# Attention in clusters and a softplus FFN: first batch by two heads, weight steps on either of two engines, one matmul for two in most similarities

## The chip, the cores and the metric

The kernel runs on one core of a Trainium2 chip. The core has a matrix engine (PE, with a weight load of its own, PEld), three engines for elementwise work (DVE, ACT, POOL) and a queue engine (SP); each takes its instructions in the order in which they were written, and they wait for each other by semaphores. DMAs are issued from the queues of ACT (loads) and SP (transposes and stores). PE writes only to PSUM, eight banks of 2 KB per partition; the other data lie in SBUF. The metric is the device time in microseconds, the median of several runs.

## The reference

Attention with 4 batches, 8 heads, 768 rows and a head size of 64, masked so that a query sees only the keys of its own cluster (16 centroids a head), then a feed-forward layer with softplus:

```python
q_assign = np.argmax(np.einsum('bhsd,hcd->bhsc', q_n, c_n), axis=-1)
k_assign = np.argmax(np.einsum('bhsd,hcd->bhsc', k_n, c_n), axis=-1)
mask = q_assign[:, :, :, None] == k_assign[:, :, None, :]
scores = np.where(mask, scale * np.matmul(q, k.transpose(0, 1, 3, 2)), -1000000000.0)
attn = softmax(scores)                      # minus the row's maximum, sum + 1e-9
x = np.matmul(attn, v)                      # then (4 * 768, 512)
h = x @ w_in                                # 512 to 2048
out = softplus(h) @ w_out                   # 2048 to 512
```

The inputs are float32, the two weights float64.

## The kernel before

Numbers are split into two float16 halves (a rounded value and what is left over), so that a float32 product is three float16 matmuls.

The work goes by *passes*: a batch has 6 blocks of 128 rows, a pass takes 3 of them for all 8 heads, so there are 8 passes, two a batch. A pass has 24 *tiles* (head by block). For a tile, `scores` (L529) makes the scores in PSUM (`s`, 4 matmuls at L544), takes the row's negative maximum on DVE (L560), and the exponential on ACT (L568). In pass 0 the result `p` is transposed by PE in float32 (`pT`, L585), copied out by ACT and DVE (L591, L593), and `attend` (L629) multiplies it with the raw v (L647). In later passes ACT rounds `p` (L607), POOL subtracts (L609, `phl`), a DMA transposes two tiles at a time, and L651 to L653 multiply. Two heads make a pair: DVE divides (L678), ACT and POOL split (L685, L687, `xn`), and a DMA transposes to `xT`.

Behind that runs the FFN of each pass: `ffn1` (L706) makes 16 column blocks `h` (L720 to L722), `softplus` (L731) turns them into `gh` through DVE (L739, L751), ACT (L741, L742, L762) and POOL (L763), and `ffn2` (L769) makes the output (L784 to L786) for two halves of the columns, with `store` (L793) behind it. `ffn1(0)` needs the `xT` of all four pairs of pass 0.

*Preparation.* `prep_k` (L412) takes two heads: load, split (ACT L423, POOL L425, `kn`), transposes (`turn`, L365: by PE and L376 in batch 0, by DMA from then on), `nearest` (L385: 12 blocks of two accumulating matmuls each, L394 and L395, with 16 columns, then four short DVE operations L399 to L403), a mask behind the copy of k in `n2`, and transposes again. `clusters` (L452) finds by a matmul with ones which clusters have any key at all (`alive`, event `al`). `prep_q` (L467) does the like for four heads and the 3 blocks of a pass; it waits for `kn` of the next pair before its load, and ahead of `nearest` for `al` of all four heads. `scores` waits for k of its pair and q of its four heads.

*Weights.* The float64 weights are made float16 halves in 32 steps (`prep_weights`, L270): 16 for `w_in`, 16 for `w_out`. A step loads 128 x 512 numbers, and then: ACT takes the absolute value of the high word scaled (L303), DVE shifts it left by 3 (L305), joins the sign (L309) and the upper bits of the low word (L315), ACT rounds (L318), POOL subtracts (L319). The raw words lie in rooms of `wo` that are still free.

*Order.* No hardware or compiler orders this. A planner in Python (`Order`, L28) runs all the generators against a model of the engines: each `op` names its engine and a duration, the planner takes the operation that can start first (then by priority, a number in units of tiles), and emits it. So every engine's queue has the order of the model. `ring(tag, n)` makes a generator wait until a buffer of n is free; `shared=True` keeps DVE and POOL operations of that kind apart in the model. In PSUM, `ps_s` has two buffers of two banks, `ps_h` two, `ps_o` and `ps_m` one each.

Of the kernel before, what the change touches and what calls it, by code (L numbers as in the profile page):

```python
# [19 lines left out]
DDS = 1024  # L20
LAG = 4
AHEAD = 10
NPE = 8
# [4 lines left out]
class Order:  # L28
# [8 lines left out]
    def __init__(self):  # L37
        self.free = dict.fromkeys(self.LAT, 0.0)
        self.ev, self.blocked, self.active = {}, {}, []
        self.dma = 0.0  # L40
        self.shared = {"DVE": 0.0, "POOL": 0.0}
        self.rings = {}
        self.cur, self.seq = None, 0
# [7 lines left out]
    def get(self, tag, size):  # L51

        k = self.rings.get(tag, 0)
        self.rings[tag] = k + 1
        return ("wait", (tag, k - size)) if k >= size else None, (tag, k)
# [23 lines left out]

    def run(self):  # L80
        while self.active:
            best = None
            for ch in self.active:
                _, eng, ns, _, opt = ch["op"]
                start = max(ch["now"], self.free[eng])
                if opt.get("shared"):
                    start = max(start, self.shared["POOL" if eng == "DVE" else "DVE"])
                prio = ch["prio"]() if callable(ch["prio"]) else ch["prio"]
                key = (start, prio, ch["seq"])
                if best is None or key < best[0]:  # L90
                    best = key, ch
            (start, _, _), ch = best
            self.active.remove(ch)
            _, eng, ns, emit, opt = ch["op"]
            self.free[eng] = start + ns
            if opt.get("shared"):
# [12 lines left out]
def tile_cluster_attention__then__softplus_ffn(  # L109
# [18 lines left out]
    SH = S // 2  # L128
    QT = 3

    passes = [(b, c0) for b in range(B) for c0 in range(0, NT, QT)]
    NF = DFF // P
    SCALE = 1.0 / math.sqrt(D)
    nb = QT * P

# [66 lines left out]

    def load(dst, src, nbytes):
        return op("ACT", 60, lambda: nc.scalar.dma_start(dst, src), dma=nbytes / 290.0)

    def flip(dst, src, blocks):

        return op(
            "SP", 150 * blocks + 100, lambda: nc.sync.dma_start_transpose(out=dst, in_=src), dma=180.0 * blocks
# [5 lines left out]
    def prep_centroids():  # L215
# [8 lines left out]
        yield op("DVE", 150, lambda: V.tensor_tensor(sq, cf, cf, ALU.mult), dma=0)  # L224
# [45 lines left out]
    def prep_weights(step: int):  # L270
# [30 lines left out]
        if f >= 0 and f // 2 in rooms:  # L301
            yield wait("wr", rooms[f // 2])
        yield op("ACT", 630, lambda: nc.scalar.activation(mag, val, AF.Abs, scale=sc))  # L303
        od.set(("wd", step))
        yield op("DVE", 420, lambda: nc.vector.tensor_scalar(mab, mab, 3, None, ALU.logical_shift_left), shared=True)  # L305
        yield op(
            "DVE",
            680,
            lambda: nc.vector.scalar_tensor_tensor(high, high, -0x80000000, mab, ALU.bitwise_and, ALU.bitwise_or),  # L309
            shared=True,  # L310
        )
# [6 lines left out]
        yield op("ACT", 610, lambda: nc.scalar.copy(part[:, 0], val))  # L318
        yield op("POOL", 1160, lambda: nc.gpsimd.tensor_tensor(part[:, 1], val, part[:, 0], ALU.subtract), shared=True)  # L319
# [11 lines left out]
    def raw_tile(nm, n, shape):  # L331

        if n < H and nm != "q":
# [3 lines left out]
        return key, p2.tile(shape, F32, tag="raw", name=f"raw{nm}_{n}")  # L337

    raw_v = {}

    def prep_v(n: int):
# [10 lines left out]
        yield op(  # L352
            "POOL",
            1640,
            lambda: nc.gpsimd.tensor_tensor(vb[:, :, :, :D], vf, vb[:, :, :, D : 2 * D], ALU.subtract),
            shared=True,
        )
# [7 lines left out]
    def turn(dst, src, name: str, on_chip: bool):  # L365
# [4 lines left out]
        for g in range(0, dst.shape[1], NT):  # L370
            hk = yield from ring("h", 2)
            ps = ps_h.tile([P, NT, P], F16, tag="h", name=f"{name}_{g}")

            def emit(g=g, ps=ps):
                for c in range(NT):
# [3 lines left out]
            if g:  # L379
                yield op("DVE", 950, lambda g=g, ps=ps: nc.vector.tensor_copy(dst[:, g : g + NT], ps))  # L380
            else:
# [500 lines left out]
```

## Time and profile before

| | us |
|---|---|
| median of 3 runs | 907.32 |
| lowest, highest | 904.31, 907.42 |
| the profiled execution | 904.0 |
| its span, first to last instruction | 902.2 |

Views of the profile used below: the page's busy times; the busy time of each engine by stretches; groups of instructions by line (count, total busy time, mean of one, idle time of the engine just before them and who ended it); the timeline (start, length, engine, line, operands); the waits by engine; and the chain of waits that ended last. PE's matmuls overlap each other, so the time that one adds is read from the distance of two starts, not from its length.

### The profile page before, as it was taken

The page shows a single profiled execution, that of the slowest core. Times are in us where ns is not written, and L with a number is a line of the kernel's source. Part 1 is how long each engine was busy: PE and PEld are TensorE (multiplying, and loading weights), DVE is VectorE, ACT ScalarE, POOL GpSimd, SP SyncE. Part 2 cuts the span into 40 slices and gives each one's busy share as a digit, 9 for nine tenths or more (in the row PEclk, how much of TensorE's full clock was granted, in tenths as well). Part 3 has the DMA queues.
Part 4 walks back from the last instruction along what each step waited for, and adds up shares of the span by engine and source line. Part 5 has one row for each costly group of instructions (what it writes and reads, how often), then busy time and mean ns, then how long its engine had stood idle before and what let it go on. Part 6 is the DMA issues. An engine that isn't in the chain of part 4 may idle for free.

```text
span 902.2 us, 19238 instructions
## 1 busy us (share of the span) xinstructions
PE 823.7 (91%) x7843; PEld 520.0 (58%) x7843; DVE 560.8 (62%) x1034; ACT 589.4 (65%) x904; POOL 523.9 (58%) x353
## 2 busy tenths in 40 slices
PE   2669797889679999999999999999999999999996
PEld 2558684555335666666666666666666666655542
DVE  5889787778685665675766666666665645433331
ACT  5657477886458877876767777867677676633320
POOL 5233326896548778777677676776676565512210
PEclk9979699999799999999999999999999999999998
DMA  6323439999546979999888779998867755600000
GB/s 222 95 94 120 130 128 195 199 226 237 141 123 159 202 171 202 223 203 230 157 199 179 162 149 206 207 211 182 171 155 161 133 115 138 126 9 25 12 1 35
DMA packets 393320, 136.02 MB, mean 151 GB/s; under 512 B 369680, under 2 KB 386064, under 8 KB 393232
## 3 DMA queue, kind: packets, MB, share of 16 engines
q1 hardware_dynamic: 371472, 99.15, 54.9%
q10 hardware_dynamic: 21760, 35.66, 13.0%
q8 instruction: 61, 1.00, 0.5%
q14 instruction: 27, 0.22, 0.1%
HBM read 35.68 MB, written 6.29 MB: 47 GB/s over the span
## 4 chain that ended last, share of the span: by engine, by line
PE 72%; DMA 4%; DVE 3%; POOL 3%; issue 2%; ACT 2%; POOLq 0%; DVEq 0%; ACTq 0%
PE s L544 10%; PE o L786 9%; PE o L784 9%; PE o L785 9%; PE h L720 8%; PE h L722 8%; PE h L721 8%; PE av L651 3%; PE av L653 3%; PE av L652 3%; DMA pt<-phl 3%; POOL phl L609 2%; DMA xT<-xn 1%; ACT p L568 1%; DVE negm L560 1%
## 5 line engine op out<-in xcount | busy, mean ns | idle before, releaser
L609 POOL TENSOR_TENSOR phl<-p,phl 128x768 f16<-128x768 f32 x168 | 277.2, 1666 | 90.9 <-ACT phl L607 54.2
L560 DVE TENSOR_REDUCE negm<-s 128x1 f32<-128x768 f32 x192 | 182.9, 954 | 67.5 <-PE s L544 65.2
L568 ACT ACTIVATE p<-s,negm 128x768 f32<-128x768 f32 x192 | 172.3, 898 | 72.9 <-DVE negm L560 47.7
L763 POOL TENSOR_TENSOR gh<-fg,gh 128x768 f16<-128x768 f32 x64 | 105.7, 1652 | 134.5 <-ACT gh L762 134.0
L720 PE MATMUL h<-xT,wi 128*128 128x384 f16 x512 | 167.9, 328 | 14.6 <-DVE fg L751 6.2
L722 PE MATMUL h<-xT,wi 128*128 128x384 f16 x512 | 168.1, 328 | 0.0
L721 PE MATMUL h<-xT,wi 128*128 128x384 f16 x512 | 168.0, 328 | 0.0
L544 PE MATMUL s<-kt,qt 128*128 128x384 f16 x768 | 158.5, 330 | 10.2 <-ACT p L568 10.0
L784 PE MATMUL o<-wo,gh 128*128 128x512 f16 x384 | 146.3, 381 | 4.9 <-ACT gh L762 3.3
L786 PE MATMUL o<-wo,gh 128*128 128x512 f16 x384 | 146.5, 382 | 1.4 <-POOL gh L763 1.4
L785 PE MATMUL o<-wo,gh 128*128 128x512 f16 x384 | 146.4, 381 | 0.1
L741 ACT ACTIVATE fa<-fa 128x384 f32<-128x384 f32 x128 | 66.6, 521 | 114.8 <-DVE fa L739 114.1
L607 ACT CAST phl<-p 128x768 f16<-128x768 f32 x168 | 134.1, 827 | 7.1 <-DMA pt<-phl 5.5
L739 DVE TENSOR_SCALAR fa<-h 128x384 int32<-128x384 int32 x128 | 71.1, 556 | 104.0 <-PE h L722 102.8
L651 PE MATMUL av<-vb,pt 128*128 128x65 f16 x1008 | 108.7, 192 | 1.9 <-DMA pt<-phl 1.8
L652 PE MATMUL av<-vb,pt 128*128 128x64 f16 x1008 | 108.7, 192 | 0.0
L653 PE MATMUL av<-vb,pt 128*128 128x65 f16 x1008 | 108.4, 194 | 0.0
L544 PEld LDWEIGHTS <-qt 128*128 128x128 f16 x768 | 72.7, 99 | 58.5 <-issue 15.1
L751 DVE SCALAR_TENSOR_TENSOR fg<-h,fa 128x384 f32<-128x384 f32 x128 | 70.6, 552 | 57.1 <-ACT fa L742 54.5
L651 PEld LDWEIGHTS <-pt 128*128 128x128 f16 x1008 | 93.6, 98 | 15.7 <-DMA pt<-phl 3.4
L652 PEld LDWEIGHTS <-pt 128*128 128x128 f16 x1008 | 92.9, 97 | 11.8
L653 PEld LDWEIGHTS <-pt 128*128 128x128 f16 x1008 | 93.1, 97 | 0.0
(114 smaller groups left out, 1193.6 us busy)
## 6 DMA issues: line engine op xcount, KB each, us to landing
wo<-in_moe_w_in_dram ACTq DMA_DIRECT2D x16, 512.0 KB, 3.6
wo<-in_moe_w_out_dram ACTq DMA_DIRECT2D x14, 512.0 KB, 3.9
rawk<-in_k_dram ACTq DMA_DIRECT2D x16, 384.0 KB, 4.8
rawv<-in_v_dram ACTq DMA_DIRECT2D x16, 384.0 KB, 4.8
rawq<-in_q_dram ACTq DMA_DIRECT2D x16, 384.0 KB, 4.2
out_dram<-ot SPq DMA_DIRECT2D x24, 256.0 KB, 2.5
pt<-phl SPq DMA_TRANSPOSE x84, 5.5
wraw<-in_moe_w_out_dram ACTq DMA_DIRECT2D x2, 512.0 KB, 3.7
```

Of the source, the lines that this page charges most:

```text
L544: nc.tensor.matmul(st[:, j, :SH], qt[:, s, i], kt[:, s, NT // 2 * j : NT // 2 * (j + 1)], start=(s == 0), stop=(s == 1),)
L560: yield op("DVE", 950, lambda: nc.vector.tensor_reduce(negm, st[:, :, :SH], AX.XY, ALU.max, negate=True))
L609: "POOL", 1640, lambda: nc.gpsimd.tensor_tensor(phl[:, u, 1], p32, phl[:, u, 0], ALU.subtract), shared=True
L651: nc.tensor.matmul(av, pt[:, 0, c], vb[:, c, D : 2 * D + 1], start=(c == 0), stop=False)
L652: nc.tensor.matmul(av[:, :D], pt[:, 0, c], vb[:, c, :D], start=False, stop=False)
L653: nc.tensor.matmul(av, pt[:, 1, c], vb[:, c, D : 2 * D + 1], start=False, stop=(c == NT - 1))
L720: nc.tensor.matmul(hp, w[0], x[0], start=(c == 0), stop=False)
L721: nc.tensor.matmul(hp, w[0], x[1], start=False, stop=False)
L722: nc.tensor.matmul(hp, w[1], x[0], start=False, stop=(c == NP - 1))
L784: nc.tensor.matmul(po, g[0], wo[:, f, 0, 0], start=(f == f0), stop=False)
L785: nc.tensor.matmul(po, g[0], wo[:, f, 0, 1], start=False, stop=False)
L786: nc.tensor.matmul(po, g[1], wo[:, f, 0, 0], start=False, stop=(f == f0 + NF // 2 - 1))
```

## The change

It has these parts.

1. **First batch by two heads.** `first_q` loads q for four heads without the wait for `kn` and spawns `prep_q` twice, for two heads each; `scores` in pass 0 waits for its two. In pass 0 `prep_q` waits for `al` only ahead of the last steps that use it. k and its mask in batch 0 share one tile of 192 columns (`kn12`, in buffers of `xT` and `phl`), which saves the copy L431. The PSUM tiles of this preparation may take any of the four pools (`EARLY`), those of `pT` two (`PTB`).
2. **Either of two engines.** An operation may name two engines, and the planner takes the one that ends sooner, with a handicap in ns: copies out of PSUM (`evict`: ACT or DVE), subtractions of a split (`sub`: POOL or DVE, handicap 2000 for DVE), and the weight steps (scale on ACT or POOL, sign on DVE or POOL, rounding on ACT or DVE). Where POOL makes the sign it multiplies by 0.0, and L309's successor shifts and joins in one operation.
3. **Weight steps by tiles.** Step s waits for the scores of tile int(1.4 s).
4. **One matmul for two** in 8 of the 12 blocks of `nearest` after batch 0 (k) and after pass 0 (q): one matmul with 32 columns (both halves of the centroids side by side) in place of two accumulating ones with 16, and one DVE sum of 256 columns for the eight.
5. **The last `xT` of pass 0** is transposed by PE in place of the DMA.
6. The planner's model: loads and DMA transposes have queues of their own, and several durations differ. `clusters` counts on the mask itself.

The core of the diff:

```diff
+FIRST = 3
+SLACK = 0
+BIAS = 2000
+WBIAS = -500
+EARLY = "homs"
+PTB = "ho"
...
+                    _, ns, eng = min((self.start(ch, e) + n + (e != eng[0]) * ch["op"][4].get("bias", 0), n, e) for e, n in zip(eng, ns))
...
-            if "dma" in opt:
-                self.dma = max(self.dma, start + 900) + opt["dma"]
-                end = max(self.dma, start + ns) + 1500
+            if "flip" in opt:
+                self.flips = max(self.flips, start + 900) + opt["flip"] * (2.0 if self.loads > start else 1.0)
+                end = max(self.flips, start + ns) + 1200
+            if "load" in opt:
+                self.loads = max(self.loads, start + 1200) + opt["load"] * (2.0 if self.flips > start else 1.0)
+                end = self.loads + 1200
...
+    def evict(dst, src, size):
+        return op(
+            ("ACT", "DVE"),
+            (180 + size * 0.8, 160 + size * 1.04),
+            (lambda: nc.scalar.copy(dst, src), lambda: nc.vector.tensor_copy(dst, src)),
+        )
+    def sub(dst, a, b, size):
+        return op(
+            ("POOL", "DVE"),
+            (150 + size * 1.95, 120 + size * 1.08),
+            [lambda e=e: e.tensor_tensor(dst, a, b, ALU.subtract) for e in (nc.gpsimd, nc.vector)],
+            shared=True,
+            bias=BIAS,
+        )
...
-        yield op("ACT", 630, lambda: nc.scalar.activation(mag, val, AF.Abs, scale=sc))
+        gate = int(WGATE + step * WPACE)
+        if gate >= 0:
+            yield wait("sc", gate)
...
+            if e == "ACT":
+                nc.scalar.activation(mag, val, AF.Copy, scale=sc)
+            else:
+                nc.gpsimd.tensor_scalar(mag, val, sc, None, ALU.mult)
+        yield op(("ACT", "POOL"), (630, 1000), [lambda e=e: scaled(e) for e in ("ACT", "POOL")], shared=True, bias=WBIAS)
...
+            if e == "POOL":
+                nc.gpsimd.tensor_scalar(val, val, 0.0, None, ALU.mult)
+            else:
+                nc.vector.tensor_scalar(mab, mab, 3, None, ALU.logical_shift_left)
+        yield op(("DVE", "POOL"), (420, 1000), [lambda e=e: signed(e) for e in ("DVE", "POOL")], shared=True, bias=WBIAS)
+        def joined():
+            if how[1] == "POOL":
+                a, x, f, b = mab, 3, ALU.logical_shift_left, high
+            else:
+                a, x, f, b = high, -0x80000000, ALU.bitwise_and, mab
+            nc.vector.scalar_tensor_tensor(high, a, x, b, f, ALU.bitwise_or)
...
+                if c < twin:
+                    nc.tensor.matmul(both[:, c], x, cents[:, 0 : low + 1 : low, h], start=True, stop=True)
+                    continue
                 nc.tensor.matmul(sim[:, c], x, cents[:, 0, h], start=True, stop=False)
                 nc.tensor.matmul(sim[:, c], x, cents[:, low, h], start=False, stop=True)
...
+    def first_q(n: int):
+        qkey[n, 0] = yield from ring("qt", 2)
+        nt = passes[0][2]
+        rk, qf = yield from load_q(n, 0)
+        qt = p2.tile([P, 2, 4, nt, P], F16, tag="qt", name=f"qt_{n}_0")
+        for u in range(4):
+            qT[n + u, 0] = qt[:, :, u]
+        for u in (0, 2):
+            od.spawn(prep_q(n + u, 0, 2, qf[:, u : u + 2], qt[:, :, u : u + 2], rk if u else None), od.cur["prio"] + u * nt)
...
-        yield wait("q", n - n % 4, pi)
+        yield wait("q", n - n % (4 if pi else 2), pi)
...
-        yield flip(
-            xT[pi][:, pr].rearrange("p s c t -> p (s c) t"), t_.rearrange("p s c d -> p (s c d)"), 2 * QT
-        )
+        yield from turn(
+            xT[pi][:, pr].rearrange("p s c t -> p (s c) t"),
+            t_.rearrange("p s c d -> p (s c) d"),
+            f"xT_{pr}_{pi}",
+            pi == 0 and pr == NP - 1,
+        )
```

More of the change, by code (lines that the diff above doesn't have):

```diff
@@ L78, in pump, with start @@
         self.cur = outer
+    def start(self, ch, eng):
+        t = max(ch["now"], self.free[eng])
+        if ch["op"][4].get("shared") and eng in self.shared:
+            t = max(t, self.shared["POOL" if eng == "DVE" else "DVE"])
+        return t
     def run(self):
         while self.active:
-            best = None
+            ready = []
             for ch in self.active:
[L84 to L87, printed above, removed]
+                eng, ns = ch["op"][1:3]
+                if isinstance(eng, tuple):
+                    _, ns, eng = min((self.start(ch, e) + n + (e != eng[0]) * ch["op"][4].get("bias", 0), n, e) for e, n in zip(eng, ns))
@@ L88, in run @@
                 prio = ch["prio"]() if callable(ch["prio"]) else ch["prio"]
[L89 to L92, printed above, removed]
+                ready.append((self.start(ch, eng), prio, ch["seq"], eng, ns, ch))
+            soon = min(ready, key=lambda r: r[:3])
+            start, _, _, eng, ns, ch = min(
+                (r for r in ready if r[3] == soon[3] and r[0] <= soon[0] + SLACK), key=lambda r: (r[1], r[0], r[2])
+            )
@@ L317, in prep_weights @@
         )
-        yield op("ACT", 610, lambda: nc.scalar.copy(part[:, 0], val))
-        yield op("POOL", 1160, lambda: nc.gpsimd.tensor_tensor(part[:, 1], val, part[:, 0], ALU.subtract), shared=True)
+        yield op(
+            ("ACT", "DVE"),
+            (610, 620),
+            (lambda: nc.scalar.copy(part[:, 0], val), lambda: nc.vector.tensor_copy(part[:, 0], val)),
+            shared=True,
+        )
+        yield sub(part[:, 1], val, part[:, 0], WC)
         od.set(("wr", step))
@@ L433, in prep_k @@
         h = n % H
         yield wait("cents")
-        hk = yield from ring("h", 2)
-        ps, sim, best = yield from nearest(
-            [kt0[:, c] for c in range(2 * NT)], [h] * NT + [h + 1] * NT, 2, f"k{n}"
-        )
-        eq = p2.tile([P, 2 * NT, NCL], F16, tag="eq", name=f"eq_k{n}")
-        yield op("DVE", 345, lambda: nc.vector.tensor_tensor(eq, sim, best, ALU.is_equal))
-        yield op(
-            "DVE",
-            250,
-            lambda: nc.vector.tensor_scalar(n2[:, :, D : D + NCL], eq, 1.0, MASK, ALU.subtract, ALU.mult),
-            shared=True,
-        )
@@ L447, in prep_k @@
-        od.spawn(clusters(n, ps, eq, hk), od.cur["prio"])
-        yield from turn(kt[:, 1].rearrange("p h c t -> p (h c) t"), n2, f"kT1_{n}", n < NPE)
-        od.set(n2k)
+        hk, ps = yield from bank(EARLY if n < H else "h", [P, 2 * (TWIN + NT), NCL], F32, f"sim_k{n}")
+        sim, best = yield from nearest(
+            ps, [kt0[:, c] for c in range(2 * NT)], [h] * NT + [h + 1] * NT, 2, f"k{n}", TWIN * (n >= H)
+        )
+        yield op("DVE", 345, lambda: nc.vector.tensor_tensor(sim, sim, best, ALU.is_equal))
@@ L450, in prep_k, with clusters @@
+        mask = n2[:, :, D : D + NCL]
+        yield op("DVE", 345, lambda: nc.vector.tensor_scalar(mask, sim, 1.0, MASK, ALU.subtract, ALU.mult))
+        od.spawn(clusters(n, ps, mask, hk), od.cur["prio"])
+        yield from turn(kt[:, 1].rearrange("p h c t -> p (h c) t"), n2, f"kT1_{n}", n < H)
+        for key in keys:
+            od.set(key)
         od.set(("k", n))
[L452 removed]
+    def clusters(n, ps, mask, hk):
         h = n % H
[L455 to L456 removed]
+        cnt = ps[:, : 2 * NT]
+        yield op("PE", 100, lambda: nc.tensor.matmul(cnt, ones, mask, start=True, stop=True))
```

300 lines of the change are left out of this document (164 added, 136 removed).

## The prediction

> **What bounds the kernel now.** I read the page's first line of busy times, then the busy time by stretches. Its columns: the stretch, its length, the busy time of PE, weight load, DVE, ACT and POOL (instructions in brackets), granted clock, DMA share, GB/s.
>
> ```profile
> PE 823.7 (91%) x7843; PEld 520.0 (58%) x7843; DVE 560.8 (62%) x1034; ACT 589.4 (65%) x904; POOL 523.9 (58%) x353
> ...
> 0.00:28.00 28.00, 9.57 (x110) 7.91 (x111) 16.20 (x61) 15.78 (x23) 14.71 (x17) 1.00 0.54 181
> 28.00:53.00 25.00, 12.70 (x181) 10.99 (x180) 21.87 (x54) 12.44 (x19) 7.93 (x6) 0.85 0.37 119
> 53.00:135.00 82.00, 72.76 (x543) 61.25 (x542) 71.63 (x116) 54.08 (x109) 22.93 (x20) 0.88 0.40 119
> 135.00:225.00 90.00, 76.15 (x828) 48.30 (x826) 68.78 (x115) 70.21 (x107) 71.58 (x47) 1.00 1.03 213
> 225.00:270.00 45.00, 30.49 (x259) 17.68 (x258) 32.05 (x66) 23.08 (x37) 20.67 (x14) 0.85 0.51 131
> 270.00:870.00 600.00, 599.29 (x5838) 364.23 (x5837) 344.84 (x618) 409.41 (x606) 382.82 (x248) 1.00 0.74 154
> ```
>
> The 91% of the first row hides two different stages. From 270 to 870 us PE is busy for 599.29 of 600 us at clock 1.00, and no other engine is over 70%: only less PE work brings time there. Before 270 us PE is idle for 270 - (9.57 + 12.70 + 72.76 + 76.15 + 30.49) = 68.3 us, and part of what it does runs at 0.85 to 0.88. All of PE's work has to be done at some time, so an idle microsecond saved before 270 comes off the end. Nearly the whole question lies in these 270 us.
>
> What holds PE there? The timeline of PE, around the first scores and at the end of pass 0:
>
> ```profile
> 44.02 0.17 PE L395 MATMUL sim_q<-cents,qt 128*128 128x16 f16 x1
> ...
> 44.52 0.17 PE L395 MATMUL sim_q<-cents,qt 128*128 128x16 f16 x1
> 49.85 0.82 PE L376 MATMUL qT<-eye,n 128*128 128x128 f16 x6 [5.16 <-POOL n L516]
> ...
> 54.03 2.27 PE L544 MATMUL s<-kt,qt 128*128 128x384 f16 x8
> ...
> 133.05 1.45 PE L647 MATMUL av<-rawv,ptf 128*128 128x64 f32 x12
> 134.33 0.50 PE L585 MATMUL pT<-eye,p 128*128 128x128 f32 x3
> 134.67 0.81 PE L544 MATMUL s<-kt,qt 128*128 128x384 f16 x4
> 135.32 1.45 PE L647 MATMUL av<-rawv,ptf 128*128 128x64 f32 x12
> ```
>
> The first scores come at 54.03 us, after the preparation of four heads. The 24 tiles of pass 0 then take until 135, 3.4 us each. By the starts in the last four rows PE needs 1.28 us a tile for `av`, 0.34 twice for `pT` and 0.65 for `s`: 2.61, or 63 us for 24. So PE alone does not set this stage; DVE is nearly full (21.87 of 25 us, 71.63 of 82). Its groups from 20 to 135 us (count, busy us, mean ns, idle before):
>
> ```profile
> L560 DVE TENSOR_REDUCE negm<-s 128x1 f32<-128x768 f32 x25 | 23.6, 948 | 3.8 <-PE s L544 3.6
> L315 DVE SCALAR_TENSOR_TENSOR wo<-wo 128x512 int32<-128x512 int32 x21 | 17.6, 836 | 0.2
> ...
> L309 DVE SCALAR_TENSOR_TENSOR wo<-wo,wi 128x512 int32<-128x512 int32 x16 | 12.4, 775 | 0.3
> L305 DVE TENSOR_SCALAR wi<-wi 128x512 int32<-128x512 int32 x16 | 10.0, 626 | 0.1
> L309 DVE SCALAR_TENSOR_TENSOR wo<-wo 128x512 int32<-128x512 int32 x5 | 3.5, 694 | 0.4
> ...
> L305 DVE TENSOR_SCALAR wo<-wo 128x512 int32<-128x512 int32 x5 | 2.1, 421 | 0.8 <-ACT wo L303 0.8
> ```
>
> Weight steps take 17.6 + 12.4 + 10.0 + 3.5 + 2.1 = 45.6 us of DVE for 21 steps, more than the scores' own reduction. That is the load the change touches.
>
> **The change part by part.** First, stage 1, up to the end of pass 0.
>
> *Start by two heads.* In the run of before, the first pair of k heads has its last transposes and copy here, and q is loaded late:
>
> ```profile
> 11.93 0.37 ACTq L204 DMA_DIRECT2D rawq<-in_q_dram  x1
> ...
> 22.95 0.80 PE L376 MATMUL kT<-eye,n 128*128 128x128 f16 x6 [0.89 <-ACT kt L382]
> ...
> 23.78 0.80 ACT L382 COPY kt<-kT 128x768 f16<-128x768 f16 x1 [0.89 <-PE kT L376]
> ```
>
> k of heads 0 and 1 is thus ready at 24.6 us. With q loaded without the wait for `kn`, prepared for two heads, and waiting for `al` only ahead of its last steps, the first scores can follow at about 28 us instead of 54. That saves no work: the other three k pairs and q halves now run between tiles. It fills PE's and POOL's idle time of 28 to 53 us. Halving q doubles its short DVE operations (two more sets of nine; at half the columns each is some 0.25 instead of 0.35 us, so 0.15 a pair is lost): 2.7 us on DVE.
>
> *Weight steps.* Step s now waits for tile int(1.4 s), so 17 steps fall into pass 0's tiles instead of 21; the sign may go to POOL, which leaves two DVE operations. The units, with L315's shortest, median and longest, and one of the short operations:
>
> ```profile
> L315 DVE SCALAR_TENSOR_TENSOR wo<-wo x30: 677/693/2159, 25.9 to 257.9; 128x512 int32<-128x512 int32 x30
> ...
> L319 POOL TENSOR_TENSOR wi<-wo,wi 128x512 f16<-128x512 f32 x16 | 18.7, 1170 | 58.2 <-ACT wi L318 58.2
> ...
> L303 ACT ACTIVATE wi<-wo 128x512 f32<-128x512 f32 x16 | 10.8, 678 | 6.1 <-DMA wo<-in_moe_w_in_dram 6.1
> ...
> L170 POOL CAST eye<-eye 128x128 f32<-128x128 f16 x1 | 0.3, 290 | 0.1
> ...
> L399 DVE TENSOR_REDUCE mx_q<-sim_q 128x12 f32<-128x192 f32 x16 | 5.6, 352 | 4.0 <-PE sim_q L395 4.0
> ```
>
> POOL's product with a number on 512 columns is not in the trace. Four times L170 gives 1.16 us, L319 with its two inputs 1.17; a cost per element below L170's, if some of that is start-up, could bring 0.6. I take 1.0, as the nearest row is L170. On DVE a step costs between 2 x 0.69 = 1.4 us (sign on POOL, nothing waits) and 45.6 / 21 = 2.2 (as now); I take 1.7. DVE's load up to 135 us is 16.20 + 21.87 + 71.63 = 109.7; it becomes 109.7 - 45.6 + 17 x 1.7 + 2.7 = 95.7. DVE was idle for 28 - 16.20 = 11.8 us at the start, which stays, and I leave 6 us of later waiting (it had 82 - 71.63 = 10.4 after 53 us): pass 0 ends at 95.7 + 18 = 114 instead of 135. PE's need fits under that: 9.57 + 12.70 of preparation and 63, in 114 us. **Stage 1 gains 21 us.** Ends: 8 (each step as dear as 2.2, and 10 us more waiting) and 30 (1.4 a step, and as much PE work as 95% of the time after 28 us can hold).
>
> *The last `xT` of pass 0 by PE.* The chain of waits holds the DMA transpose, and PE's wait list for 135 to 290 us shows what it cost:
>
> ```profile
> 144.97 8.12 DMA xT<-xn
> ...
> PE s L544 <- ACT p L568: 8.9, 9, 1.8
> PE h L720 <- DVE fg L751: 6.2, 4, 3.3
> PE h L720 <- DVE aq L511: 5.4, 1, 5.4
> PE h L720 <- DMA xT<-xn: 2.9, 1, 2.9
> ```
>
> Of the 8.12 us PE idled 2.9, the rest lay under score and `av` work. Six transposes (0.80 in the row at 22.95) and two copies replace it: 0 to 8 us, and I take **2.9**.
>
> *One matmul for two.* Twelve k and fourteen q preparations lose 8 matmuls each, 208 in all. Twenty starts lie between 44.02 and 44.52, 25 ns each, and with 32 columns one is still at the short end. 208 x 0.025 = **5.2 us** off PE, nearly all in the full stretch. The added DVE sum (26 on 256 columns, 0.47 us each by L399's 352 ns on 192) lies beside PE there, where DVE has 345 of 600 us; without that cover it would cost 12. That covers as well the copies and splits that may now run on either engine.
>
> *Pass 1 and the change of batch*, 135 to 270 us: 15 weight steps are left instead of 11, free to use any engine, while `phl`, `gh` and `kn` splits may leave POOL when it is behind. The new order may close some of the waits listed, or make others. Ends: 14 gained (half of the idle 135 - 76.15 - 30.49 = 28.4) and 40 lost (below); I take 0, as the load per engine stays near what it is.
>
> Sum: 21 + 2.9 + 5.2 + 0 = 29 us. The profiled execution took 904.0 us with a span of 902.2, which is the low end of the three runs (904.3 to 907.4, median 907.3). 904.0 - 29 = **875 us**; against the median it would be 878.
>
> **The rivals.** *DVE is held by POOL.* L315 takes 677 ns at best and 836 on average over the 21 above, though POOL is busy for only 22.93 of 82 us. The excess, with L309's 775 - 694 and L305's 626 - 421, is 0.45 us a step. With 17 steps of up to 3.2 us (1.0 + 1.0 + 1.17) POOL would be busy for some two thirds of the stage, 2.4 times the share, and two operations would then wait 1.1 us a step: DVE 2.5 a step, 13 us more than my 1.7. Gain 8 + 2.9 + 5.2: 888 us. The Trainium skill, SBUF — State Buffer, "SBUF: two separate sides", says that DVE in some modes and GpSimd take one pair of ports by an exclusive lock for a whole instruction, so that the other waits; by that rule the steps handed to POOL come back as DVE waits. The trace agrees in kind (677 against 2159 ns for one form), not yet in amount.
>
> *The change of batch closes too.* If k and q of batch 1 come early enough, the 14 us come on top: 861 us, or 852 if stage 1 also gives 30. For it: the waits on `fg` and `aq` are queue order, not load. Against it: k of batch 1 still waits for the buffers of batch 0.
>
> *POOL becomes the bound of pass 1 (slower).* The stretch again, for L319 alone (length, POOL's busy time):
>
> ```profile
> 135.00:225.00 90.00, 8.10 (x7) 1.00 1.03 213
> ```
>
> POOL has 71.58 of 90 us there, of which L319 is 8.1. Fifteen steps at 3.2 us are 48: 111 us of POOL, and with the idle 18.4 kept the stage lasts 130 instead of 90. 904 - 29 + 40 = 915 us. It decides from 29 us more POOL work, (29 + 8.1) / 15 = 2.5 us a step, that is when POOL does more than half of both optional operations. Against it: either engine may take them.
>
> *It does nothing measurable.* The first q half still comes only after all k heads, because of queue order, and pass 1 gives back the DVE relief: 900 to 910.
>
> **How the numbers follow.** Forecast (862 to 884) 0.46; DVE held 0.18 (884 to 900); the change of batch too 0.20 (848 to 862); nothing 0.06; slower 0.10. The range 851 to 902 leaves out the slower case, the nothing case's upper part and a sliver below: 2 in 10. About 0.5% of 907.3, 4.5 us, is what a measurement of this kernel can tell from no change. Faster 0.84, same 0.06, slower 0.10.
>
> **What would show it.** Right: first scores near 28 us, pass 0's last near 114, PE full from some 245 us on, sim matmuls 208 fewer. Wrong: first scores after 40; L309 and L315 means over 1.0 us (DVE held); POOL over 95% between pass 0 and the full stretch, with PE waiting for `p` (the slower rival); a longer stretch of scores missing at the change of batch.

## The result, and the profile after

The changed kernel takes 937.47 us (median of 4 runs, 936.91 to 938.79) against 906.42 for the kernel before (4 runs): a ratio of 1.0348, 95% interval 1.0324 to 1.0372. It is slower by 3.5%, where 875 us and a gain had been forecast. The span of the profiled execution is 936.7 us, 34.5 more than before. Every time given below is the median of all runs of a kernel; a ratio with its interval leaves out the runs that took over 1.5% more than the fastest of the same kernel (four of e11's ten, one of e19's eight).

The page's first line, and the busy time by the same stretches as in the prediction (length, PE, weight load, DVE, ACT, POOL, clock, DMA share, GB/s), for the changed kernel:

```profile
PE 840.9 (90%) x7641; PEld 525.0 (56%) x7641; DVE 561.7 (60%) x1045; ACT 583.2 (62%) x907; POOL 588.3 (63%) x397
...
0.00:28.00 28.00, 10.53 (x148) 8.97 (x148) 15.03 (x70) 13.97 (x22) 13.73 (x19) 1.00 0.55 182
28.00:53.00 25.00, 19.44 (x194) 14.63 (x195) 20.53 (x54) 20.13 (x41) 19.87 (x16) 0.80 0.30 104
53.00:135.00 82.00, 73.65 (x532) 64.98 (x531) 55.88 (x89) 50.06 (x98) 48.70 (x36) 0.88 0.36 89
135.00:225.00 90.00, 65.70 (x616) 39.54 (x614) 71.28 (x105) 60.69 (x93) 76.95 (x51) 0.81 0.94 203
225.00:270.00 45.00, 37.99 (x381) 22.15 (x377) 36.63 (x67) 29.56 (x44) 36.92 (x25) 0.96 0.95 199
270.00:330.00 60.00, 48.60 (x445) 29.08 (x443) 37.53 (x69) 36.79 (x58) 43.22 (x30) 0.94 0.77 145
330.00:660.00 330.00, 318.19 (x3214) 194.25 (x3212) 198.63 (x375) 229.34 (x338) 225.93 (x146) 0.99 0.95 179
```

The stretch that the prediction showed as one, full from 270 us on, is split here. The same two rows of the kernel before:

```profile
270.00:330.00 60.00, 59.40 (x618) 36.54 (x617) 35.73 (x60) 47.34 (x68) 47.10 (x31) 1.00 0.84 182
330.00:660.00 330.00, 329.89 (x3515) 206.17 (x3514) 212.29 (x394) 247.08 (x361) 239.22 (x155) 1.00 0.92 189
```

Up to 53 us PE has more to do than before. In pass 1 it has less: 65.70 instead of 76.15 of 90 us, and at clock 0.81 instead of 1.00. From 225 to 270 us it has more (37.99 for 30.49), then less again: 48.60 instead of 59.40 of 60, and 318.19 instead of 329.89 of 330. PE is no longer full where it had been full, and no other engine is full in its place: from 330 to 660 us ACT is busiest of the others, at 229 of 330.

Busy time hides part of this: at half clock matmuls start twice as far apart (0.32 us against 0.162 for `h`, in the timeline below), and PE counts as busy all the while. So PE's lost time was counted: from each stretch the number of starts of each form is taken, times the distance that two starts of that form have at full clock (scores and `h` 0.162 us, `o` 0.216, `av` 0.030, in pass 0 0.112, `pT` 0.110, similarities 0.025; other transposes at 0.070, between the two distances 0.056 and 0.107 at which they stand), and what is left of the stretch is lost.

| PE lost, us | 0-53 | 53-135 | 135-270 | 270-330 | 330-660 | 660-end | sum |
|---|---|---|---|---|---|---|---|
| before | 39 | 19 | 37 | 1 | 2 | 13 | 111 |
| after | 32 | 20 | 49 | 17 | 17 | 16 | 151 |

PE's work by the same count went from 790.8 to 786.0 us. The 34.5 us of span are thus 39.3 more lost and 4.8 less work (the sum must come out, as the loss is what the count leaves). Of the loss 12 us arise between 135 and 270 us, and 31 between 270 and 660.

What PE waits for there, between 135 and 660 us (line, what it waits for: us in all, times, longest; `p` are the exponentials, `pt` their transposed split, `fg` and `gh` belong to softplus, `n` is the masked half of k), after:

```profile
PE s L666 <- ACT p L690: 17.3, 13, 3.8
PE av L769 <- DMA pt<-phl: 15.0, 8, 3.4
PE h L840 <- DVE fg L872: 6.4, 5, 3.7
PE o L908 <- POOL gh L240: 4.0, 1, 4.0
PE sim_k L544 <- DVE n L533: 3.8, 3, 2.0
PE sim_k L473 <- DVE fg L872: 3.5, 1, 3.5
```

In the list of before, quoted in the prediction, the first is 8.9, and the second has this row:

```profile
PE av L651 <- DMA pt<-phl: 1.8, 2, 1.3
```

Over the whole there is no one wait to blame: several, on four different partners, grew together. (From 330 to 660 us it is nearly one alone, that for `pt`; see the numbers of the planner below.) In each an operation stands in PE's queue before its data are there, and holds up what comes behind it. What a long one costs beyond itself is seen in the timeline after (start, length, line, operands, in brackets the idle time before):

```profile
216.20 0.38 PE L906 MATMUL o<-wo,gh 128*128 128x512 f16 x1
216.42 0.38 PE L907 MATMUL o<-wo,gh 128*128 128x512 f16 x1
220.75 0.39 PE L908 MATMUL o<-wo,gh 128*128 128x512 f16 x1 [3.95 <-POOL gh L240]
220.97 0.38 PE L906 MATMUL o<-wo,gh 128*128 128x512 f16 x1
221.19 0.59 PE L907 MATMUL o<-wo,gh 128*128 128x512 f16 x1
221.58 0.63 PE L908 MATMUL o<-wo,gh 128*128 128x512 f16 x1
...
223.41 0.52 PE L842 MATMUL h<-xT,wi 128*128 128x384 f16 x1
223.73 0.52 PE L840 MATMUL h<-xT,wi 128*128 128x384 f16 x1
```

After 3.95 us without work the starts of `o` lie first 0.22 us apart, then 0.39, and those of `h` behind them 0.32 where they had lain 0.162 apart: the clock falls to about half shortly after the stall. The Trainium skill, TensorE: Matmul & The Clock Gate, "Part 1: The HAM clock gate", says that the clock has two steps only, full and half, and that an idle window of some 3.4 us brings the half one; this trace agrees, with 0.32 against 0.162 us and a stall of 3.95 us.

### The profile page after: what moved, and what is told of

Read it like the earlier page. It is cut to its first block, busy times and chain, and to the rows that moved or that the text cites. A ratio compares the mean times of both kernels' runs of the same rounds, so it can differ in the third digit from the quotient of the medians.

```text
span 936.7 us, 18935 instructions
## 1 busy us (share of the span) xinstructions
PE 840.9 (90%) x7641; PEld 525.0 (56%) x7641; DVE 561.7 (60%) x1045; ACT 583.2 (62%) x907; POOL 588.3 (63%) x397
## 4 chain that ended last, share of the span: by engine, by line
PE 66%; DMA 9%; POOL 8%; DVE 7%; issue 4%; ACT 4%; ACTq 1%; POOLq 0%; SPq 0%; DVEq 0%
PE s L666 9%; PE o L906 8%; PE o L908 8%; PE o L907 8%; DMA pt<-phl 7%; PE h L840 7%; PE h L842 6%; PE h L841 6%; POOL phl L240 5%; PE av L765 4%; PE av L769 2%; PE av L771 2%; PE av L770 2%; DVE negm L682 2%; ACT p L690 1%
## 5 line engine op out<-in xcount | busy, mean ns | idle before, releaser
L666 PE MATMUL s<-kt,qt 128*128 128x384 f16 x768 | 164.2, 339 | 21.7 <-ACT p L690 21.3
L240 POOL TENSOR_TENSOR gh<-fg,gh 128x768 f16<-128x768 f32 x64 | 107.6, 1683 | 115.3 <-ACT gh L883 115.1
L906 PE MATMUL o<-wo,gh 128*128 128x512 f16 x384 | 149.1, 388 | 5.1 <-ACT gh L883 3.3
L908 PE MATMUL o<-wo,gh 128*128 128x512 f16 x384 | 148.7, 387 | 4.6 <-POOL gh L240 4.6
L907 PE MATMUL o<-wo,gh 128*128 128x512 f16 x384 | 148.9, 388 | 0.0
L769 PE MATMUL av<-vb,pt 128*128 128x65 f16 x1008 | 112.3, 195 | 15.8 <-DMA pt<-phl 15.8
L860 DVE TENSOR_SCALAR fa<-h 128x384 int32<-128x384 int32 x128 | 71.0, 555 | 92.1 <-PE h L842 91.4
L769 PEld LDWEIGHTS <-pt 128*128 128x128 f16 x1008 | 95.6, 100 | 33.3 <-DMA pt<-phl 20.8
L770 PE MATMUL av<-vb,pt 128*128 128x64 f16 x1008 | 112.3, 195 | 0.0
L771 PE MATMUL av<-vb,pt 128*128 128x65 f16 x1008 | 112.0, 197 | 0.0
L770 PEld LDWEIGHTS <-pt 128*128 128x128 f16 x1008 | 95.2, 99 | 12.1 <-issue 0.7
L771 PEld LDWEIGHTS <-pt 128*128 128x128 f16 x1008 | 95.2, 99 | 0.0
```

The costliest lines, as they stand in the source:

```text
L240: [lambda e=e: e.tensor_tensor(dst, a, b, ALU.subtract) for e in (nc.gpsimd, nc.vector)],
L666: nc.tensor.matmul(st[:, j, :SH], qt[:, s, i], kt[:, s, NT // 2 * j : NT // 2 * (j + 1)], start=(s == 0), stop=(s == 1),)
L769: nc.tensor.matmul(av, pt[:, 0, c], vb[:, c, D : 2 * D + 1], start=(c == 0), stop=False)
L770: nc.tensor.matmul(av[:, :D], pt[:, 0, c], vb[:, c, :D], start=False, stop=False)
L771: nc.tensor.matmul(av, pt[:, 1, c], vb[:, c, D : 2 * D + 1], start=False, stop=(c == NT - 1))
L906: nc.tensor.matmul(po, g[0], wo[:, f, 0, 0], start=(f == f0), stop=False)
```

## The experiments

Two families of theories were tried. In the one, a part of the change costs the time: the product on POOL, the later weight steps, the planner's DMA model, the added DVE sum. In the other the instructions are worth what the prediction said or near it, and the time goes with the order that the planner makes of them, which any change of any number remakes. Each kernel ran beside the kernel before on the same chip, and ratios are to that.

### Parts of the change taken back (e1 to e3)

e1 gives the planner the one queue for loads and transposes that the kernel before had:

```diff
-            if "flip" in opt:
-                self.flips = max(self.flips, start + 900) + opt["flip"] * (2.0 if self.loads > start else 1.0)
-                end = max(self.flips, start + ns) + 1200
-            if "load" in opt:
...
+            if "flip" in opt or "load" in opt:
+                self.flips = max(self.flips, start + 900) + opt.get("flip", 0) + opt.get("load", 0)
+                end = max(self.flips, start + ns) + 1500
...
-flip=148.0 * blocks
+flip=180.0 * blocks
```

> The changed kernel with the planner's DMA model of before: loads and transposes in one queue, 180 ns a block, 1500 ns after the end. Theory A (the new model lands transposes too early, so that av and the next scores stand in PE's queue ahead of their data): PE's wait of av for pt falls from 15.8 us to under 4 and the time to 905 or less. Theory B (weight steps on POOL fill pass 1) and theory C (the weight steps come too late) both expect 930 to 942, with pass 1's scores still taking some 92 us.

e2 fixes the engines: scale and rounding on ACT, the sign on DVE, every split on POOL.

```diff
-BIAS = 2000
+BIAS = 10**9
...
-        yield op(("ACT", "POOL"), (630, 1000), [lambda e=e: scaled(e) for e in ("ACT", "POOL")], shared=True, bias=WBIAS)
+        yield op("ACT", 630, lambda: scaled("ACT"))
...
-        yield op(("DVE", "POOL"), (420, 1000), [lambda e=e: signed(e) for e in ("DVE", "POOL")], shared=True, bias=WBIAS)
+        yield op("DVE", 420, lambda: signed("DVE"), shared=True)
```

> The changed kernel with scale and rounding of a weight step on ACT, the sign on DVE and every split's subtraction on POOL, as before. Theory B: POOL's 77 of 90 us between 135 and 225 falls by 15 or more, pass 1's scores take 75 us or less instead of 92, and the time is 905 to 915. Theories A and C: 930 to 942, and pass 0 up to 5 us longer, since DVE gets the sign back.

e3 unties the weight steps from the tiles and gives them the priorities of before:

```diff
-        if gate >= 0:
+        if gate >= 10**6:
...
-        od.spawn(prep_weights(step), WGATE + WDUE + step * WPACE)
+        od.spawn(prep_weights(step), begin[0] - 12 + step * 0.6)
```

> The changed kernel with the weight steps not tied to tiles, at the priorities of before (some 22 of 32 done by the end of pass 0). Theory C: pass 1's scores take 75 us or less, the time is 905 to 915. Theories A and B: 930 to 942; by B, pass 0 is longer too, because the steps' POOL work lies there.

Measured: e1 921.09 us, ratio 1.0144 (1.0004 to 1.0284); e2 933.91, 1.0285 (1.016 to 1.0411); e3 938.81, 1.0339 (1.0214 to 1.0464). The row of e2 for pass 1:

```profile
135.00:225.00 90.00, 66.20 (x627) 40.99 (x625) 69.68 (x113) 64.96 (x100) 62.89 (x43) 0.83 0.96 200
```

POOL has 62.89 us there instead of 76.95, and PE is as empty as before the edit: POOL's load was not the bound. The old DMA model brought half the loss back, with a wide interval. e3 was a bad test: without the tie only 10 of the 32 weight steps were done by 135 us, against 14 after and 20 before, so it made them later and not earlier.

### The matmul for two alone (e4, e8, e5)

e4 is the kernel before with the one matmul for two; e8 the changed kernel without it; e5 is e4 with the DVE sum and the maximum behind it emitted as one operation, so that the planner sees nothing new and keeps every queue in the order of before.

```diff
+                if c < twin:
+                    nc.tensor.matmul(both[:, c], x, cents[:, 0 : low + 1 : low, h], start=True, stop=True)
+                    continue
...
-        yield op("DVE", 345, lambda: nc.vector.tensor_reduce(mx, sim, AX.X, ALU.max))
+        def summed():
+            if twin:
+                nc.vector.tensor_reduce(sim[:, :twin], both.rearrange("p c s l -> p c l s"), AX.X, ALU.add)
+            nc.vector.tensor_reduce(mx, sim, AX.X, ALU.max)
+        yield op("DVE", 345, summed)
```

> The kernel before with one change: one matmul for two in 8 of 12 blocks of the similarities after the first pass. All theories: 4 to 5 us less than before (208 matmuls at 25 ns), so 901 to 903, if the order of the rest stays as dense.

> The changed kernel with two matmuls for every block again. Theory E: 915 to 922, the loss of e4_twin undone. Theory D: between 925 and 945, since the order is a new one and the DMA model is still that of the change.

> The kernel before with one matmul for two, and the added DVE sum issued with the maximum behind it, unseen by the planner, so that every queue keeps the order of before. Theory D (the chip's cost of the edit is a gain of 4 to 5 us; the 17 us that e4_twin lost come from another order of the queues): 901 to 904. Theory E (the edit itself is dear, by the added DVE sum in the chain that leads to the masks): 915 to 923, as e4_twin.

Measured: e4 922.9, 1.0164 (1.0037 to 1.029); e8 928.8, 1.0259 (1.0119 to 1.0399); e5 907.79, 1.0015 (0.9964 to 1.0065), its profiled span 900.6 against 902.2. The same matmuls and sums thus cost 16 us in an order that the planner made for them and nothing measurable in the order of before. PE has 5.2 us less to do in e5 (790.8 to 785.6, counted with the forecast's own 25 ns a matmul), but the time does not show it: 907.79 us lies between what the two theories had expected, and the interval leaves room for a gain of 3 us at most.

### The order alone (e6, e7)

The kernel before with one number of the planner changed. No matmul or elementwise operation is added or taken away; only the order in the queues can be another.

```diff
-        yield op("DVE", 950, lambda: nc.vector.tensor_reduce(negm, st[:, :, :SH], AX.XY, ALU.max, negate=True))
+        yield op("DVE", 954, lambda: nc.vector.tensor_reduce(negm, st[:, :, :SH], AX.XY, ALU.max, negate=True))
```

> The kernel before with one number of the planner's model changed by 0.4% (954 ns in place of 950 for the row maximum), which moves few instructions. Theory D: some other time than before, 905 to 920. Theory E: 904 to 908.

```diff
-dma=180.0 * blocks
+dma=178.0 * blocks
```

> The kernel before with another number changed by 1% (178 ns a block in place of 180 for DMA transposes), which moves most of PE's queue. The same work with the same instructions. Theory D (the order of before is a dense one that a change of any number breaks): 912 to 925. Theory E, and whoever thinks that such orders are equal: 903 to 909.

Measured: e6 906.12, 1.0009 (0.9983 to 1.0035); e7 924.25, 1.0209 (1.01 to 1.0318). In e6 the traces show on every engine the sequence of names and shapes that before has, so it repeats the order of before and tests no other. In e7 45% of the places in PE's queue hold another name or shape. A number changed by 1% thus costs 2% of the time. The row of e7 where before has PE at 59.40 and clock 1.00:

```profile
270.00:330.00 60.00, 52.63 (x524) 31.58 (x523) 39.33 (x69) 39.58 (x60) 40.95 (x27) 0.94 0.70 164
```

Seven of the microseconds are missing at the place where the change lost eleven of busy time. Among its neighbours the order of before is a good one.

### Numbers of the planner, one at a time (e9, e12, e14 to e17)

e9 is the changed kernel with the true length of `av` in pass 0; e12 the kernel before with the change's DMA model.

```diff
-        yield op("PE", 680 if pi == 0 else 530, emit)
+        yield op("PE", 1300 if pi == 0 else 530, emit)
```

> The changed kernel with the planner told that av of a tile in pass 0 takes 1300 ns, as before and as the trace shows (1.28 us), in place of 680. Theory G (the loss comes from this one wrong number): 905 to 912. Theory D (every such number only picks another order, and most orders lose against the one of before): 915 to 940.

```diff
-                self.dma = max(self.dma, start + 900) + opt["dma"]
-                end = max(self.dma, start + ns) + 1500
+                self.dma = max(self.dma, start + 900) + opt["dma"] * (2.0 if self.loads > start else 1.0)
+                end = max(self.dma, start + ns) + 1200
...
-dma=180.0 * blocks
+dma=148.0 * blocks
```

> The kernel before with nothing but the change's DMA model in the planner (transposes and loads in two queues, 148 ns a block, 1200 ns after the end). Theory A (this model lets PE run up against transposes that have not landed): PE waits over 10 us for pt, 920 to 940. Theory D: some time from 905 to 930, with or without that wait.

Measured: e9 939.76, 1.0367 (1.0286 to 1.0447), no help; e12 921.58, 1.0166 (1.0098 to 1.0234). In e12 PE's wait for `pt` grew from 1.8 us to this:

```profile
PE av L654 <- DMA pt<-phl: 10.7, 6, 5.4
```

So the theory came up that the new model places `av` too close behind the landing of its transpose: of 168 tiles, 30 after (8 before) have `av` less than 1 us behind it. e14 tests that with later landings in the model, e15 by starting `attend` two tiles later, e16 by both together; e17 gives later landings to the kernel before.

```diff
-                self.flips = max(self.flips, start + 900) + opt["flip"] * (2.0 if self.loads > start else 1.0)
-                end = max(self.flips, start + ns) + 1200
+                self.flips = max(self.flips, start + 900) + opt["flip"] * (1.3 if self.loads > start else 1.0)
+                end = max(self.flips, start + ns) + 2700
...
-flip=148.0 * blocks
+flip=180.0 * blocks
```

> The changed kernel, the planner told that transposes land late: 180 ns a block, 1.3 times that beside loads, 2700 ns after the end. Theory J (the changed orders lose because av, and the scores that follow it in PE's queue, stand too close behind the landing of their data): av behind landing by under 1 us in at most 12 of 168 tiles (30 in the change), PE's wait for pt under 6 us (15.8), time 895 to 918. Theory D alone (any order is a draw, with no one cause): 915 to 940 and no relation to that count.

```diff
-LAG = 4
+LAG = 6
```

> The changed kernel with av of a tile given a priority 6 tiles behind its scores instead of 4. Theory J: only a priority, while the planner still believes in early landings, so little: 920 to 940. If the distance by priority were what matters: 895 to 915.

> The changed kernel with both of these, the true 1300 ns for av in pass 0 and 300 ns behind PE: all numbers of time that e13 has, with the weight steps' pace and the PSUM banks of the change. Theory J: 885 to 910. If e13's gain came from the pace of the weight steps and the banks: 915 to 935.

```diff
-    LAT = {"PE": 200, "DVE": 60, "ACT": 60, "POOL": 60, "SP": 0}
+    LAT = {"PE": 300, "DVE": 60, "ACT": 60, "POOL": 60, "SP": 0}
...
-                end = max(self.dma, start + ns) + 1500
+                end = max(self.dma, start + ns) + 2700
```

> The kernel before with 2700 ns in place of 1500 behind a DMA and 300 in place of 200 behind PE in the planner. If e13's gain over before were late landings alone, this one would gain as well: 885 to 900. Theory J: before has the distance already (8 of 168 tiles under 1 us), so nothing is won, 900 to 925; what e13 has over before is the earlier start and the saved matmuls.

Measured: e14 932.04, 1.0285 (1.0225 to 1.0345); e15 945.68, 1.0435 (1.0352 to 1.0519); e17 920.51, 1.0158 (1.0106 to 1.0209). e16 (which also has the numbers of e9 and PE's 300) gave 1003.89 and 914.19 in its two executions, so it settles nothing. e14 speaks against the theory in this form: only 10 tiles are left with less than 1 us, and yet:

```profile
PE av L769 <- DMA pt<-phl: 16.5, 6, 5.9
```

The wait is as long as after (15.0) in fewer and longer pieces, so the number of tiles close behind a landing is not what costs. e15 lies above both of its ranges.

By stretch, though, the planner's DMA model does show, and the count by tiles hid it. From 330 to 660 us the eight kernels with the change's model (after, e2, e3, e8, e9, e12, e15, e18) lose 6 to 18 us of PE's time, 13 on the mean; the eleven with another (before, e1, e4 to e7, e11, e13, e14, e17, e19) lose 2 to 9, 4 on the mean. The wait for `pt` in that stretch, after and in e12:

```profile
PE av L769 <- DMA pt<-phl: 9.4, 4, 3.4
PE av L654 <- DMA pt<-phl: 8.2, 4, 5.4
```

Before and e1 have no such wait there. e14 has 3.0, but from 135 to 270 us it has 11.4, where after has 2.5. So the model of part 6 costs some 9 us of that stretch by the means, in the change's instructions and in before's alike, though each kernel is a single order and chance is in each; from 270 to 330 us it does not help to take it back, as e1 loses 21 us there.

### Orders picked by replaying them (e11, e13)

If the order is what costs, a better one may exist for the same work. The planner's constants were searched, and each order was replayed with durations taken from the traces rather than the planner's. Replayed so, before came out at 914 us and after at 923, so the replay has the sign right and too little of the size. Two of the best orders ran. e13:

```diff
-WGATE = 0
-WPACE = 1.4
-WDUE = 4
-LAG = 4
+WGATE = -4
+WPACE = 1.0
+WDUE = 0
+LAG = 6
...
-BIAS = 2000
-WBIAS = -500
-EARLY = "homs"
-PTB = "ho"
+BIAS = 4000
+WBIAS = 500
+EARLY = 'hom'
+PTB = 'h'
```

with the DMA numbers of e14, the 1300 of e9 and PE's 300. e11 has WPACE 1.1, WDUE 0, WBIAS 100000, 1300 for `av`, and other latencies.

> The changed kernel, its instructions nearly the same, with planner numbers picked for their order: each order was replayed with the traces' durations, in-order queues and transposes that land as late as in the traces (by that replay before is 914, the change 923, this one 888). In it scale and sign of the weight steps stay on ACT and DVE, the first batch starts by two heads, and one matmul stands for two. Theory D: faster than before, 880 to 900, with PE idle for less than 10 us between 270 us and the end of the scores. Theory H (something in the change's own instructions costs the time, whatever the order): 915 or more.

> The same with another set of numbers, that leaves the weight steps the choice of POOL and has 6 tiles from a tile's scores to its av in place of 4 (by the replay 882 to 910). Theory D: 880 to 912. Theory H: 915 or more.

Measured: e11 901.98 (896.6 over the six runs of its ratio), 0.9868 (0.9818 to 0.9918); e13 894.39, 0.9868 (0.9794 to 0.9942). Both are some 1.3% faster than the kernel before, and 35 to 43 us faster than the changed kernel. They have the start by two heads, the steps by tiles and the matmul for two; the product on POOL is hardly taken (none in e11, whose handicap rules it out, one in e13, 38 after). Taking it back alone, in e2, was worth 3.6 us. Rows of e13, from the fastest of its four executions (888.3 us):

```profile
135.00:225.00 90.00, 77.07 (x782) 47.97 (x782) 72.09 (x122) 67.94 (x105) 73.57 (x48) 0.96 1.07 205
225.00:270.00 45.00, 34.73 (x325) 21.06 (x326) 34.98 (x62) 30.39 (x44) 27.95 (x18) 0.89 0.86 186
270.00:330.00 60.00, 60.00 (x631) 37.92 (x629) 37.79 (x64) 45.81 (x69) 43.85 (x30) 1.00 0.98 178
330.00:660.00 330.00, 328.10 (x3366) 202.81 (x3363) 216.14 (x416) 244.78 (x361) 236.98 (x155) 1.00 1.00 187
```

PE is full again from 270 us on. But e13 still waits 10.0 us for `pt`, longer than before, 8.5 of them ahead of 270 us: a faster time does not need every wait gone.

### The pace of the weight steps (e18, e19)

e13 has 19 weight steps done by 135 us, the changed kernel 14. e18 gives the changed kernel the quicker pace alone; e19 gives e13 the slower one back.

```diff
-WGATE = 0
-WPACE = 1.4
-WDUE = 4
+WGATE = -4
+WPACE = 0.9
+WDUE = 0
```

> The changed kernel with the weight steps tied to earlier tiles (step s to tile 0.9 s - 4 in place of 1.4 s) and spawned with an earlier priority. Theory K (the weight steps come too late: 14 of 32 are done by 135 us in the change, 20 before, 19 and 20 in the two picked orders, and the rest collides in pass 1 with splits, transposes and the next batch's k): 17 to 20 steps done by 135 us, pass 1's scores end by 208, time 905 to 922. Theory D alone: 925 to 945, since only the order is another.

> The picked order e13 with the weight steps' pace of the change (tile 1.4 s, and its priority). Theory K: some 15 steps done by 135 us, and 15 us or more of e13's gain gone, 905 to 925. If the pace does not matter: 885 to 900, if its draw is as good, and nothing in the count of steps would go with the time.

Measured: e18 930.66, 1.0256 (1.0102 to 1.0411), with 17 steps done; e19 910.28, 1.0023 (0.9986 to 1.006), with 15 steps (one of its eight executions took 4153.9 us, for which no cause was seen; the other seven lie between 904.58 and 912.74). The slow pace costs 16 us in the picked order. In the change's own order the quick one is worth 7, which the interval does not tell from nothing: it wins 11 us of PE's time from 270 to 330 us and loses 3 from 135 to 270. The pace is one contributor, and not the cause.

PE's lost time for the kernels that tell most, counted as above:

| | time | 0-53 | 53-135 | 135-270 | 270-330 | 330-660 | 660-end |
|---|---|---|---|---|---|---|---|
| e7, before's work, another order | 924.25 | 39 | 21 | 35 | 12 | 7 | 15 |
| e12, the same | 921.58 | 40 | 18 | 39 | 3 | 14 | 15 |
| e5, the matmul for two, order of before | 907.79 | 39 | 18 | 40 | 0 | 3 | 14 |
| e1, after with the old DMA model | 921.09 | 31 | 22 | 40 | 21 | 2 | 15 |
| e19, picked, slow pace | 910.28 | 26 | 19 | 45 | 6 | 6 | 14 |
| e18, after with the quick pace | 930.66 | 34 | 19 | 52 | 6 | 18 | 17 |
| e11, picked | 901.98 | 33 | 20 | 42 | 1 | 2 | 15 |
| e13, picked | 894.39 | 35 | 15 | 31 | 0 | 4 | 14 |

Every kernel here over 915 us loses 16 to 24 us between 270 and 660 (e17, not shown, 15), and the others 3 to 13. The start of the kernel hardly tells them apart.

## Why the prediction was wrong

**What failed: "*Pass 1 and the change of batch* ... I take 0", and with it the sentence on 270 to 870 us, "only less PE work brings time there".** The full stretch was treated as a property of the kernel. It is a property of one order of its queues. The reason given for the 0, "as the load per engine stays near what it is", was true as far as it goes and beside the point: what leaves PE empty is the place of each operation in its queue, and the change remade every queue. The range given for that step, 14 gained to 40 lost, holds the 12 lost from 135 to 270 us; the 31 lost behind 270 had no term at all. e7 shows that a new order alone does this to unchanged instructions, and e5 that an unchanged order keeps the loss away from one changed part, the matmul for two. Part 6 of the change, the planner's numbers, was given no term either, and its DMA model goes with some 9 us of the loss from 330 to 660 (the means of eight orders against eleven; 12 and 15 in the pairs before and e12, e1 and after).

The forecast counted 29 us gained, and the span grew by 34.5. Of these 63.5 us, 15 are stage 1, 15 lie between 135 and 270 us (where 2.9 had been counted as gained and 12 were lost), 31 between 270 and 660, and 3 behind that.

**Stage 1 gains 21 us: the earlier start came, though later than forecast; the relief of DVE brought nothing that shows.** The first scores came at 37.91 us instead of 54.03, and not at 28:

```profile
29.09 0.34 PE L454 MATMUL qT<-eye,n 128*128 128x128 f16 x3 [0.55 <-POOL n L635]
...
34.02 0.48 PE L454 MATMUL qT<-eye,n 128*128 128x128 f16 x3
...
37.91 1.49 PE L666 MATMUL s<-kt,qt 128*128 128x384 f16 x4
```

The masked half of q needs six transposes for two heads. The first three start at 29.09, the next of that form not before 34.02, behind work on k, and they and the first scores start without a wait: it is again the order of PE's queue that holds them. The timeline of DVE shows a smaller part:

```profile
12.61 3.54 DVE L599 SCALAR_TENSOR_TENSOR qn<-rawq,qn 128x384 f16<-128x384 f32 x2 [2.05 <-ACT qn L595]
```

The split of q now stands in DVE's queue among the first heads' work, where the prediction priced only the short operations of the second half; PE's transposes waited 1.1 us for it. The last `av` of pass 0, after and before:

```profile
127.76 1.45 PE L765 MATMUL av<-rawv,ptf 128*128 128x64 f32 x12
...
137.25 1.45 PE L647 MATMUL av<-rawv,ptf 128*128 128x64 f32 x12
```

It starts some 9.5 us earlier and not 21 (the prediction read the end of pass 0 as 135, and it is 138.7). From the first scores to the end of that `av` the 24 tiles take 91.3 us instead of 84.7, with the preparation of the other heads among them. DVE's load up to 135 us was forecast at 95.7 and is 15.03 + 20.53 + 55.88 = 91.4, with 14 steps done in place of 17, and a step costs DVE 23.8 / 14.5 = 1.6 us, against the 1.7 taken: the first two of these rows, from 20 to 135 us (15 and 14 steps), with two casts of 0.8 us together, make the 23.8.

```profile
L383 DVE SCALAR_TENSOR_TENSOR wo<-wi,wo 128x512 int32<-128x512 int32 x15 | 13.1, 887 | 0.3 <-POOL wo L372 0.3
L389 DVE SCALAR_TENSOR_TENSOR wo<-wo 128x512 int32<-128x512 int32 x14 | 9.9, 716 | 0.0
...
L232 DVE COPY ptf<-pT 128x384 f32<-128x384 f32 x14 | 7.6, 553 | 16.3 <-PE pT L706 16.2
```

What failed is the 18 us of idle DVE: up to the end of pass 0 at 129 us DVE is busy for 86.2, so idle for some 43 us, 16 of them ahead of the copies of `pT` (the third row; 3.3 before). DVE's load was thus not what set the length of the pass; that the chain from scores to `av` set it in its place is an inference from these waits. By PE's lost time stage 1 gave 6 us (58 to 52): 7 up to 53 us, and nothing from 53 to 135, where 19 became 20.

**POOL's product** was taken as 1.0 us between 0.6 and 1.2; it is 1.59:

```profile
L372 POOL TENSOR_SCALAR wo<-wo 128x512 f32<-128x512 f32 x22 | 34.7, 1586 | 5.2 <-ACT wi L361 3.7 <-POOL wo L240 0.6 <-POOL phl L240 0.5
L363 POOL TENSOR_SCALAR wi<-wo 128x512 f32<-128x512 f32 x7 | 11.1, 1588 | 0.0
```

That is above the upper end; but e2, where POOL makes none of them, is only 3.6 us faster than the change, so little seems to hang on it.

**The matmul for two** took 208 matmuls off PE as forecast, 5.2 us by its price, but in an unchanged order (e5) the time shows no gain. **The last `xT`** held: its wait went from 2.9 us to 1.0 (on the copy that took the DMA's place).

**The rivals.** The one on the slower side had the sign of pass 1 right (it said 40 us lost) and the mechanism wrong: POOL has 76.95 of 90 us there, not 95%, and relieving it changed nothing (e2). *DVE is held by POOL* needed means over 1.0 us; L383 has 887 in stage 1. What no rival said is that a planner's order can spoil a stage that the change doesn't touch.

**What stays open.** Before's instructions took 906 us in their own order (and in e6, which has the same) and 921 to 924 in three others (e7, e12 and e17); the change's (with e2 and e8, without e16 and e19) took 921 to 946 in nine orders that were not picked, and 894 and 902 in two that were. About 16 of the 31 us by which the medians differ thus look like the distance of any new order from the good one of before. The means of those unpicked orders, 922 and 934, leave 12 us in which something of the change makes its orders worse on the whole. The DMA model is in it, by some 9 us on the mean between 330 and 660 us in the seven of the nine that have it, and so is the pace of the weight steps (e19), though e18 shows that it is not all. These are few orders, two runs for most of them. What decides between 135 and 330 us was not settled: the DMA model, the length of `av`, the engines, and the distance from the landings each failed as the single cause. A picked order that uses the product on POOL was not tried.

## What to carry to other kernels

Where a program fixes all queues ahead by a planner, a change has two effects: the work that it removes, and a new order of everything, which here was worth more (e7: 17 us for 1% of one number, against 5 us of PE work saved). So measure the change in an unchanged order first (as e5), try changed numbers of the planner on the old kernel alone (as e12), or compare several orders on both sides, and give the reordering a term of its own in the forecast, from how far jittered orders of the old kernel scatter. A dense stretch in a profile is evidence about that order only.

## What the hardware showed beside that

- A product with a number on POOL (one input, 128 x 512 in float32) takes 1.59 us, more than the subtraction with two inputs and a float16 result on the same columns (1.17 in the rows of before).
- A matmul with 32 columns starts as often as one with 16. The group of those of q in the changed kernel has a mean length of 177 ns, and eight in a row take 0.36 us: (360 - 177) / 7 = 26 ns apart, against 25. The group, and the eight in the timeline:

```profile
L473 PE MATMUL sim_q<-cents,qt 128*128 128x32 f16 x112 | 5.0, 177 | 2.0 <-DMA qt<-qn 2.0
```

```profile
273.72 0.36 PE L473 MATMUL sim_q<-cents,qt 128*128 128x32 f16 x8 [0.56 <-DMA qt<-qn]
```

- The same DVE operation on 512 columns lasts from 677 ns to 2135 ns. The 14 that run from 151 to 277 us, where POOL is busy for 82 to 86% of the time, have a median of 1132; the 15 before, of 686. The two groups also differ in their inputs (`wi` and `wo`, or `wo` alone), and no run shows that POOL is the cause:

```profile
L383 DVE SCALAR_TENSOR_TENSOR wo<-wi,wo x15: 679/686/1957, 46.9 to 132.5; 128x512 int32<-128x512 int32 x15
L383 DVE SCALAR_TENSOR_TENSOR wo<-wo x14: 677/1132/2135, 151.8 to 276.6; 128x512 int32<-128x512 int32 x14
```
